# SyncE's queue in written order from the third pass on, and down's first load of h at the first product of the pass's last pair

## The chip, the cores and the metric

The kernel runs on one core of a Trainium2 chip. The metric is the device time of one execution in microseconds (us): 2458.67 us, median of three runs (2456.48 to 2459.65). Five engines work from their own queues: TensorE (PE; its weight loads are PEld), VectorE (DVE), ScalarE (ACT), GpSimd (POOL) and SyncE (SP). SP issues every DMA of this kernel.

## The reference, cut to what matters

```
S, D, H, Dh, F = 2048, 1024, 32, 32, 3584
xn = layernorm(x)
q, k, v = split(xn @ wqkv)                       # per head
phi(u) = concat(softmax(u @ w_phi), softmax(-(u @ w_phi)))
kv, z = phi(k)^T v, sum of phi(k) over s
o = (phi(q) kv) / (phi(q) z + 1e-6);  s = o @ wo
h = silu(xn @ w1) * (xn @ w3);        g = silu(h @ w2)
out = x + s * g
```

## The kernel before, in words

All large products are in float32 kept as two parts (a rounded high part and the rest, made by `split`, ACT for the high part and then DVE for the rest), and take three matmuls each (`PASSES`). Every 2 x 2 block product is done with seven block products, A11, A12, S2, S1, S3, S4 and A22, whose left operands are blocks of one matrix and sums of them, and whose right operands are called B11, B21, T2, T1, T3, B22 and T4.

The stages are, in order of time:

- up (to about 1175 us): h for all tokens, written to `h_d`.
- Three passes (c = 0, 1, 2; up to about 1683 us) over eight pairs of token tiles: keys and values for c = 0 and 1, queries for c = 2. A pair is seven products of 12 matmuls. `reload` brings the next pair's seven operands (tiles `xo`, L522). In the third pass `spikes` takes maxima, differences and an exponential of each result and stores it to `e_d` (L696, or L723 for two tiles, pairs 3 and 5, that are also scaled here with the tile `ee`).
- down (about 1673 to 2219 us): g = silu(h @ w2), loop `for r, new in enumerate(steps)`. Its contraction is cut in seven parts (kb = 0 to 6), and each part runs over the eight pairs (i = 0 to 7). Step r is 8 kb + i, 56 of them. `load_b(kb, n)` brings the nth right operand in two halves (tiles `bo` and `late`, L803, 512 KB each, in a ring of 24). `a_first(kb, i)` loads that step's h (tile `hr`, L810, 512 KB) and makes the high and low parts `af` (for A11 and A12) and `as2` (for S2); `a_second` makes those for S1, S3, S4 and A22 (`as`) from the same `hr`.
- In turn r of that loop PE does S1 of step r-1, A11 of r, S3 of r-1, A12 of r, S4 of r-1, S2 of r and A22 of r-1, 6 matmuls each. DVE adds each result to the accumulators `acc` (L987); A11 goes through ACT and POOL instead (L984, L985).
- In the last part (kb = 6, steps 48 to 55) `gate` applies Silu to each finished pair's two tiles on ACT (L918) and stores them (`g_d`, L919). The same turns load the weights and tiles of the last stage (`wos` L913, `zb` L731, `e` L931).
- The last stage (to 2454 us) puts s together and writes out.

What sets the order: within `in_order(...)` the named engines get their instructions as the code writes them. Outside it a scheduler places them, engine by engine, by its own costs. Up runs in order. Passes and down run scheduled on all engines until `new is None` (after step 55), from where SP, ACT, DVE and POOL are in order again, and in the last stage PE too. Whatever made the order, each engine's queue then runs strictly in it: an instruction that waits holds those behind it.

Of the kernel before, what the change touches and what calls it, by code (L numbers as in the profile page):

```python
# [28 lines left out]
def tile_kernel(ctx: ExitStack, tc: tile.TileContext, x, wkT, wqT, wv, wphi, wo, w1, w3, w2, out):  # L29
# [3 lines left out]
    def pool(name, bufs, **kw):  # L33

        open_pools[name] = tc.tile_pool(name=name, bufs=bufs, reuse_waits="tile", **kw)
        return open_pools[name].__enter__()

    def close(*names):
        for name in names:
            open_pools.pop(name).__exit__(None, None, None)  # L40

    ENG = mybir.EngineType
# [3 lines left out]
    def in_order(*engines):  # L46

        if ordered:
            ordered.pop().__exit__(None, None, None)
        if engines:  # L50
            ordered.append(tc.manual_schedule(engines=set(engines)))
            ordered[0].__enter__()
# [36 lines left out]
    def split(hi, lo, src, by=None):  # L89

        nc.scalar.copy(hi, src)  # L91
        (by or nc.vector).tensor_sub(lo, src, hi.bitcast(F))  # L92
# [66 lines left out]
    def fetch(m, j):  # L159
        t = slot(m, j)  # L160
        if m < 2:
            n = ANAMES[j]
            for q in range(4):
                nc.sync.dma_start(t[:, :, :, q * P:(q + 1) * P].bitcast(F), xo_d[m][n][:, q])
        else:
            n = BNAMES[j]
            nc.sync.dma_start(t.bitcast(F), wkv_d[m - 2][n])
        return {n: t}

    def quad(name, dt=R):  # L170
        return qp.tile([P, 2, 4, P], dt, name=name, tag="q")
# [345 lines left out]
    def reload(i, names=ANAMES):  # L517

        xo = {}
        for n in names:  # L520
            xo[n] = quad(f"xo{n}")
            nc.sync.dma_start(xo[n].bitcast(F), xo_d[i // 4][n][:, i % 4])  # L522
        return xo
# [107 lines left out]
    def seven(xo, wb):  # L631

        bank = {}
        for b, an, bn in ORDER:
# [8 lines left out]
            yield an, bank[b]  # L643

    def heads(i, xo, wb, steps, pend):

        nonlocal pkv
        first, last = i == 0, i + 1 == len(pairs)
        for an, pb in seven(xo, wb):
# [23 lines left out]
            else:  # L673
# [4 lines left out]
                kv(pkv, first, False, e0, v0)  # L678
                keys(pb, e1)
            next(steps)  # L680
        return pkv, False, last, e1, v1

# [46 lines left out]
    def load_z(two):  # L729
        for c in range(2):  # L730
            nc.sync.dma_start(two[c], z_d[:, c].rearrange("o g j s f -> o (g j s f)").to_broadcast([P, D]))  # L731

    def queries(i, xo, wb, steps, pend):

        t0, t1 = pairs[i]
# [51 lines left out]
    def ring(name):  # L787
        nonlocal ring_at
        k = ring_at % 24
        ring_at += 1  # L790
        if k < 8:
            return bpa.tile([P, 2, 512], R, name=name, tag=f"ra{k}")
        if k < 20:
            return bpb.tile([P, 2, 512], R, name=name, tag=f"rb{k}")
        return late_rw[(k - 20) // 2][:, k % 2]
# [3 lines left out]
    def load_b(kb, n):  # L799
        n = BNAMES[n]  # L800
        for kk in range(2):
            t = ring("bo")
            nc.sync.dma_start(t.bitcast(F), w2_d[kb][n][:, kk])  # L803
            bos[kb, n, kk] = t

    def a_first(kb, i):


        hq = quad("hr", F)
        nc.sync.dma_start(hq.rearrange("p b k t -> p (b k t)"),  # L810
                          h_d[i // 4][kb][i % 4].rearrange("p b h k t -> p (b h k t)"))
        hr = hq.rearrange("p b (h k) t -> p b h k t", h=2)
        sm = work.tile([P, 2, P], F, name="sm", tag="w")
        f1, f2 = quad("af"), work.tile([P, 2, 2, P], R, name="as2", tag="w")
        nc.vector.tensor_sub(sm, hr[:, 1, 0], hr[:, 0, 0])
        split(f1[:, 0], f1[:, 1], hq[:, 0])
        split(f2[:, 0], f2[:, 1], sm)
        return hq, sm, {"A11": (f1, 0), "A12": (f1, 2), "S2": (f2, 0)}

    def a_second(hq, sm, _):  # L820
        hr = hq.rearrange("p b (h k) t -> p b h k t", h=2)
        s34 = work.tile([P, 4, P], F, name="s34", tag="w")
        nc.vector.tensor_sub(s34[:, 0:2], hr[:, 1, 1], sm)
        nc.vector.tensor_sub(s34[:, 2:4], hr[:, 0, 1], sm)
        t1, t2 = quad("as"), quad("as")
        split(t1[:, 0], t1[:, 1], hq[:, 1])
        split(t2[:, 0], t2[:, 1], s34)
        return {"S1": (t1, 0), "A22": (t1, 2), "S3": (t2, 0), "S4": (t2, 2)}
# [3 lines left out]
    def split_wo(step):  # L832

        if step == 0:
            wso["room"] = [big.tile([P, 8, 512], F, name="room", tag=f"big{j}") for j in range(2)]
        for m in range(16):
            room, at_ = wso["room"][m % 4 // 2], 3 * (m % 2)
            raw_w, two = room[:, at_], room[:, at_ + 1:at_ + 3].bitcast(R)
            c, k = m // 8, m % 8
            if step == 2 * m:  # L840
                nc.sync.dma_start(raw_w, wo[k * P:(k + 1) * P, c * 512:(c + 1) * 512])
            elif step == 2 * m + 3:
                split(two[:, 0], two[:, 1], raw_w)
            elif step == 2 * m + 5:
                nc.sync.dma_start(wo_d[c][k], two.bitcast(F))
# [7 lines left out]
    ready = []  # L853
    for c in range(3):
        wbn = {}
        if c == 2:
            close("spare")
            bpa = pool("ra", 1, side="right")
        for i in range(len(pairs)):
            nxt, end = {}, i + 1 == len(pairs)  # L860

            def steps():
                for j in range(7):
                    if c == 0 and 4 <= 7 * i + j < 40:
                        split_wo(7 * i + j - 4)
                    if j == 0:
                        if i + 2 == len(pairs) and c < 2:
                            for m in range(2):
                                wbn.update(fetch(c + 3, m))
                        if not (end and c == 2):  # L870
                            nxt.update(reload((i + 1) % len(pairs)))
                        if c == 2 and i in (1, 2):
                            load_b(0, i - 1)
                        if c == 2 and end:
                            load_b(0, 2)
                            load_b(0, 3)
                    if later:
                        later.pop(0)()

                    if end and c < 2:  # L880
                        if j < 4 or (j == 4 and c == 0):
                            wbn.update(fetch(c + 3, j + 2))
                        if j == 6 and c == 1:
                            wbn.update(fetch(c + 3, 6))
                    if end and c == 2 and j in (1, 4):
                        ready.append(a_first(0, 0) if j == 1 else a_second(*ready[0]))
                    yield

            pend = (queries if c == 2 else heads)(i, xo, wb, steps(), pend)
            assert not (end and later)  # L890
            xo = nxt
        wb = wbn
# [101 lines left out]
    for r, new in enumerate(steps):  # L994
        kb, i = new or (NKB, 0)
        end = kb == NKB - 1
# [19 lines left out]
        if 8 <= r < 24:  # L1016
            c, j, s = (r - 8) // 8, (r - 8) // 2 % 4, r % 2
# [173 lines left out]
```

## Time and profile before

| | us |
|---|---|
| median of three runs | 2458.67 (2456.48 to 2459.65) |
| the profiled execution, its own time | 2455.73 |
| its span, first to last instruction | 2453.9 |
| mean granted TensorE clock | 0.995 |
| PE busy | 2380.6 (97%) |
| DVE busy | 1684.7 (69%) |
| ACT busy | 902.5 (37%) |

Idle time of PE is what is to be looked at first, since PE is busy for 97% of the span. In a timeline row the bracket tells how long the engine sat idle before it and what ended that; `x12` counts the merged instructions. A row of SP (SPq) is a DMA's issue, not its transfer.

### The profile page before, as it was taken

Reading aid. Unit: us, or ns where it says so; the run is one execution under the profiler, and the core shown is the slowest. Engines: PE = TensorE matmul, PEld = TensorE weight load, DVE = VectorE, ACT = ScalarE, POOL = GpSimd, SP = SyncE. Lnnn points to the kernel's source line nnn. Section 1 sums busy time; section 2 is a strip of 40 time slices with the busy share of each in tenths; the row PEclk is TensorE's granted clock in tenths of the full one; section 3 lists DMA queues with packets and bytes.
Section 4 is the critical chain, followed back from the end, with each engine's and each line's share of the span. In section 5 each row is a group of like instructions: output and inputs, shape, how many; then the busy total and the mean of one; then the engine's idle time right before and its main releaser. Section 6 shows DMA issues by size and latency. Waiting matters only on the chain.

```text
span 2453.9 us, 35828 instructions
## 1 busy us (share of the span) xinstructions
PE 2380.6 (97%) x13554; PEld 1951.1 (80%) x13554; DVE 1684.7 (69%) x2493; ACT 902.5 (37%) x1566; POOL 716.9 (29%) x511
## 2 busy tenths in 40 slices
PE   6999999999999999999999999998999999999999
PEld 5888877788777888878788788886888888887887
DVE  8556777775467777774476565695688787876764
ACT  6444544443344555443121111333422222243221
POOL 1233454543345565542000000010011111124653
PEclk9999999999999999999999999999999999999999
DMA  7566688966886777765998867978433444366553
GB/s 262 174 222 224 222 269 294 299 228 207 264 275 240 264 272 262 253 244 180 386 333 329 338 217 298 374 282 300 175 123 109 173 179 172 140 244 243 189 186 112
DMA packets 289548, 586.30 MB, mean 239 GB/s; under 512 B 23648, under 2 KB 138592, under 8 KB 286688
## 3 DMA queue, kind: packets, MB, share of 16 engines
q1 hardware_dynamic: 289376, 584.02, 68.2%
q8 instruction: 107, 1.75, 0.3%
q14 instruction: 65, 0.53, 0.1%
HBM read 379.19 MB, written 205.00 MB: 238 GB/s over the span
## 4 chain that ended last, share of the span: by engine, by line
PE 74%; DMA 9%; DVE 6%; issue 5%; POOL 3%; SPq 2%; ACT 1%; DVEq 0%; ACTq 0%; POOLq 0%
PE bankb L557 18%; PE bankb L975 12%; PE bankb L640 10%; PE bankc L557 8%; PE bankc L975 6%; PE banka L557 5%; PE bankc L640 5%; PE banka L975 3%; PE banka L640 2%; PE pm L1095 2%; DVE bo L92 1%; POOL ez L936 1%; POOL e L962 1%; DMA wkv_d0T<-wkvo 1%; PE pkv L626 1%
## 5 line engine op out<-in xcount | busy, mean ns | idle before, releaser
L92 DVE TENSOR_TENSOR bo<-rw,bo 128x512 fp32r<-128x512 f32 x336 | 292.6, 872 | 145.0 <-ACT bo L91 144.4
L91 ACT CAST bo<-rw 128x512 fp32r<-128x512 f32 x336 | 205.8, 621 | 49.8 <-DMA wkv_d0T<-wkvo 5.7
L985 POOL TENSOR_TENSOR acc<-acc,u 128x512 f32<-128x512 f32 x48 | 62.6, 1304 | 491.4 <-ACT u L984 491.4
L975 PE MATMUL bankb<-bo,as 128*128 128x512 f32 x816 | 200.9, 389 | 0.0
L269 POOL TENSOR_TENSOR rw<-rw,t 128x512 f32<-128x512 f32 x56 | 79.2, 1413 | 382.0 <-DVE bo L92 382.0
L1095 PE MATMUL pm<-wos,oT 128*128 128x512 f32 x768 | 183.0, 394 | 0.0
L975 PEld LDWEIGHTS bankb<-bo,as 128*128 128x128 f32 x816 | 153.2, 188 | 31.8
L557 PE MATMUL bankb<-op1A,bo 128*128 128x512 f32 x672 | 161.2, 396 | 11.5 <-DVE u L585 7.9
L557 PE MATMUL bankb<-op0A,bo 128*128 128x512 f32 x672 | 160.1, 392 | 8.6 <-DVE u L585 8.3
L1095 PEld LDWEIGHTS pm<-wos,oT 128*128 128x128 f32 x768 | 141.9, 188 | 31.7 <-issue 2.8
L557 PE MATMUL bankc<-op0S,bo 128*128 128x512 f32 x672 | 163.4, 391 | 2.0 <-ACT u L583 1.5
L557 PE MATMUL bankb<-op0S,bo 128*128 128x512 f32 x672 | 163.4, 392 | 1.8 <-ACT u L576 1.6
L557 PE MATMUL bankc<-op1S,bo 128*128 128x512 f32 x672 | 161.8, 390 | 1.6 <-ACT u L583 1.6
L557 PE MATMUL bankb<-op1S,bo 128*128 128x512 f32 x672 | 161.5, 389 | 0.0
L557 PEld LDWEIGHTS bankb<-op1A,bo 128*128 128x128 f32 x672 | 127.2, 191 | 42.4 <-DVE u L585 11.8
L557 PEld LDWEIGHTS bankb<-op0A,bo 128*128 128x128 f32 x672 | 125.1, 188 | 37.5 <-DVE u L585 11.4
L557 PEld LDWEIGHTS bankc<-op1S,bo 128*128 128x128 f32 x672 | 125.9, 188 | 28.8 <-ACT u L583 2.4
L557 PEld LDWEIGHTS bankc<-op0S,bo 128*128 128x128 f32 x672 | 125.2, 188 | 29.1 <-ACT u L583 2.4
L975 PE MATMUL bankc<-bo,as 128*128 128x512 f32 x576 | 146.6, 389 | 1.8 <-DMA bo<-w_d0B 1.8
L557 PEld LDWEIGHTS bankb<-op0S,bo 128*128 128x128 f32 x672 | 125.0, 188 | 29.0 <-ACT u L576 3.3
L557 PEld LDWEIGHTS bankb<-op1S,bo 128*128 128x128 f32 x672 | 126.0, 188 | 26.6 <-ACT u L576 0.4
L975 PEld LDWEIGHTS bankc<-bo,as 128*128 128x128 f32 x576 | 108.0, 188 | 24.9 <-DMA bo<-w_d0B 2.2
(241 smaller groups left out, 4683.4 us busy)
## 6 DMA issues: line engine op xcount, KB each, us to landing
rw<-in_w SPq DMA_DIRECT2D x112, 512.0 KB, 4.7
h_d<-h SPq DMA_DIRECT2D x112, 256.0 KB, 7.2
hr<-h_d SPq DMA_DIRECT2D x56, 512.0 KB, 3.6
xoS<-xo_d0S SPq DMA_DIRECT2D x48, 512.0 KB, 8.7
xoS<-xo_d1S SPq DMA_DIRECT2D x48, 512.0 KB, 7.7
xoA<-xo_d0A SPq DMA_DIRECT2D x36, 512.0 KB, 7.3
xoA<-xo_d1A SPq DMA_DIRECT2D x36, 512.0 KB, 5.8
e<-e_d SPq DMA_DIRECT2D x32, 512.0 KB, 4.3
```

What stands on the lines that cost most here:

```text
L91: nc.scalar.copy(hi, src)
L92: (by or nc.vector).tensor_sub(lo, src, hi.bitcast(F))
L269: nc.gpsimd.tensor_sub(b11, b22, t2)
L557: nc.tensor.matmul(bank[b], bo[bn][:, w, k], ao[an][:, u, k], start=first and n == 0, stop=LAST[b] == an and n == 11, skip_group_check=True)
L626: nc.tensor.matmul(pkv[sl, m], e[:, m // 4, (m % 4) * P + 32 * h:(m % 4) * P + 32 * h + 32], v[:, 4 * (m % 4) + h], start=first and m == 0 ...
L640: nc.tensor.matmul(bank[b], xo[an][:, u, k], wb[bn][:, w, k], start=an in ("A11", "A12", "S1") and n == 0, stop=LAST[b] == an and n == 11, ...
L936: nc.gpsimd.tensor_mul(t, es[i][c], zb[c])
L962: eng.tensor_mul(e3, e3, f.rearrange("p h s -> p (h s)").unsqueeze(2).to_broadcast([P, H, DH]))
L975: nc.tensor.matmul(bank[b], t[:, u, pos + k], bos[kb, bn, k][:, w], start=first and n == 0, stop=LAST[b] == an and n == 5, skip_group_chec ...
L985: nc.gpsimd.tensor_add(c, c, u)
L1095: nc.tensor.matmul(p, oT[k // 4][:, a, k % 4], wos[c, k][:, b], start=n == 0, stop=n == 23)
```

## The change

It puts SP, and SP alone, in written order from the start of the third pass. Since nothing ends that before `new is None`, it holds for all of down too. In the last pair of the third pass it writes step 0's load of h behind the first product instead of the second, and the loads of B right operands 2 and 3 (T2 and T1) behind the third and fourth instead of the first. The loads of operands 4 to 6 (T3, B22, T4) stay where they were written: behind the pass.

```
     for c in range(3):
         if c == 2:
+            in_order(ENG.SP)
             close("spare")
...
-                        if c == 2 and end:
-                            load_b(0, 2)
-                            load_b(0, 3)
+                    if c == 2 and end and j in (2, 3):
+                        load_b(0, j)
...
-                    if end and c == 2 and j in (1, 4):
-                        ready.append(a_first(0, 0) if j == 1 else a_second(*ready[0]))
+                    if end and c == 2 and j in (0, 4):
+                        ready.append(a_first(0, 0) if j == 0 else a_second(*ready[0]))
```

The scheduler, seeing another queue on SP, also orders ACT, DVE and PE anew. Three places matter.

SP around the end of the third pass, before. `e_d` are stores of the pass, of which `e_d_0_182` is the sixth pair's last and `e_d_0_176`, `1_185`, `1_177` and `0_184` are the last pair's four. `w_d0T_204`, `0T_205`, `0T_206`, `0B_207`, `0T_208` are T2, T1, T3, B22 and T4 of kb = 0.

```order
L696 DMA e_d_0_182<-eq 128x1024
L803 DMA bo<-w_d0T_204 128x1024 x2
L803 DMA bo<-w_d0T_205 128x1024 x2
L696 DMA e_d_0_176<-eq 128x1024
L810 DMA hr<-h_d_0_57 128x1024
L1019 DMA kvu_d<-kv_d_252 32x4x32 x8
L810 DMA hr<-h_d_0_57 128x1024 x2
L696 DMA e_d_1_185<-eq 128x1024
L803 DMA bo<-w_d0T_206 128x1024 x2
L696 DMA e_d_1_177<-eq 128x1024
L696 DMA e_d_0_184<-eq 128x1024
L803 DMA bo<-w_d0B_207 128x1024 x2
```

The first `hr` is step 0's, the next two are those of steps 1 and 2. And now:

```order
L696 DMA e_d_0_182<-eq 128x1024
L810 DMA hr<-h_d_0_57 128x1024
L696 DMA e_d_0_176<-eq 128x1024
L803 DMA bo<-w_d0T_204 128x1024 x2
L803 DMA bo<-w_d0T_205 128x1024 x2
L696 DMA e_d_1_185<-eq 128x1024
L696 DMA e_d_1_177<-eq 128x1024
L696 DMA e_d_0_184<-eq 128x1024
L803 DMA bo<-w_d0T_206 128x1024 x2
L803 DMA bo<-w_d0B_207 128x1024 x2
L803 DMA bo<-w_d0T_208 128x1024 x2
L810 DMA hr<-h_d_0_57 128x1024 x2
```

Step 0's `hr` moved up past four right-operand loads and a store. Those of steps 1 and 2 moved down, behind the pass's last store and six right-operand loads. The small `kvu_d` copies went further down, one to each turn.

SP in the turns of kb = 6, now. The first `hr<-h_d_6_63 x2` are the loads for steps 49 and 50, and the single one behind them that for step 51; `g_d_71` and `75` are the two tiles of the pair of step 48, `g_d_72` and `76` those of step 49.

```order
L810 DMA hr<-h_d_6_63 128x1024 x2
L919 DMA g_d_71<-acc_14244 128x1024
L919 DMA g_d_75<-acc_14245 128x1024
L913 DMA wos<-wo_d_0_186 128x1024
L913 DMA wos<-wo_d_1_187 128x1024
L913 DMA wos<-wo_d_2_188 128x1024
L913 DMA wos<-wo_d_3_189 128x1024
L731 DMA zb<-z_d 128x1024 x2
L810 DMA hr<-h_d_6_63 128x1024
L919 DMA g_d_72<-acc_14287 128x1024
L919 DMA g_d_76<-acc_14288 128x1024
L913 DMA wos<-wo_d_4_190 128x1024
```

Before, all three loads (steps 50, 51 and 52) stood ahead of `g_d_71`, mixed with the `wos`. Now the `hr` of step 51 stands behind the stores of step 48's pair, four `wos` and two `zb`, and in the same way that of step 52 behind the stores of step 49's pair and that of step 53 behind step 50's.

ACT in the same turns, before. `af` with its number is the high part for one step's A11: 18033 is step 51, 18122 step 52. `acc0` and `acc4` are the pair of step 48, `acc1` and `acc5` that of step 49.

```order
L91 CAST af_18033<-hr_18030 128x512
L91 CAST as2_18034<-sm_18032 128x256
L91 CAST as_18097<-hr_17941 128x512
L918 ACTIVATE acc0_14242<-acc0_14242 128x1024
L91 CAST as_18098<-s34_18094 128x512
L918 ACTIVATE acc4_14243<-acc4_14243 128x1024
L984 COPY u_18055<-bankb_18048 128x512
L91 CAST af_18122<-hr_18119 128x512
L91 CAST as2_18123<-sm_18121 128x256
L91 CAST as_18186<-hr_18030 128x512
L918 ACTIVATE acc1_14285<-acc1_14285 128x1024
L91 CAST as_18187<-s34_18183 128x512
```

And now, where `af_18035` is step 51's and `af_18124` step 52's, and `acc2` and `acc6` are the pair of step 50:

```order
L918 ACTIVATE acc4_14245<-acc4_14245 128x1024
L984 COPY u_18057<-bankb_18050 128x512
L918 ACTIVATE acc1_14287<-acc1_14287 128x1024
L918 ACTIVATE acc5_14288<-acc5_14288 128x1024
L91 CAST af_18035<-hr_18032 128x512
L91 CAST as2_18036<-sm_18034 128x256
L91 CAST as_18099<-hr_17943 128x512
L91 CAST as_18100<-s34_18096 128x512
L984 COPY u_18146<-bankb_18139 128x512
L918 ACTIVATE acc2_14366<-acc2_14366 128x1024
L918 ACTIVATE acc6_14367<-acc6_14367 128x1024
L91 CAST af_18124<-hr_18121 128x512
```

Step 51's cast stood ahead of the Silu of step 48's pair and now stands behind that of step 49's, whose second tile is complete only with A22 of step 49, the last product of turn 50. In the same way step 52's stands behind step 50's pair, and step 54's behind step 52's; steps 53 and 55 are not so placed. DVE's parts of these steps moved with them: they stand behind the adds of that same A22.

## The prediction

> **What bounds the kernel now.** I read the page's head first, then PE's waits from the third pass to the end of down, then the timelines of PE, SP, ACT and DVE round those waits, and the turns of kb = 6.
>
> ```profile
> span 2453.9 us, 35828 instructions
> PE 2380.6 (97%) x13554; PEld 1951.1 (80%) x13554; DVE 1684.7 (69%) x2493; ACT 902.5 (37%) x1566; POOL 716.9 (29%) x511
> ...
> PE bankb L975 <- ACT af L91: 9.1, 1, 9.1
> ...
> PE bankc L975 <- DMA bo<-w_d0B: 1.8, 1, 1.8
> ```
>
> PE is the bound, and down's products (L975) wait twice (us in total, times, longest): 9.1 us for the first `af`, 1.8 us for a right operand. Down has no third wait, so what the change can win there is small, and any new wait adds to the end.
>
> ```profile
> 1661.10 2.88 PE L640 MATMUL bankc<-op4T,xoS 128*128 128x512 f32 x12
> 1673.04 0.79 PE L975 MATMUL bankb<-bo,af 128*128 128x512 f32 x1 [9.07 <-ACT af L91]
> 1673.83 4.32 PE L640 MATMUL bankb<-op4T,xoS 128*128 128x512 f32 x12
> 1677.99 2.91 PE L640 MATMUL bankc<-op4B,xoS 128*128 128x512 f32 x12
> 1680.73 2.88 PE L640 MATMUL bankb<-op4T,xoA 128*128 128x512 f32 x12
> 1683.45 1.30 PE L975 MATMUL bankb<-bo,af 128*128 128x512 f32 x5
> ...
> 1696.50 2.57 PE L975 MATMUL bankc<-bo,as 128*128 128x512 f32 x10 [1.77 <-DMA bo<-w_d0B]
> 1698.90 1.07 PE L975 MATMUL bankb<-bo,af 128*128 128x512 f32 x4
> ...
> 646.88 8.40 PE L557 MATMUL bankb<-op1A,bo 128*128 128x512 f32 x24 [3.64 <-DMA op1A<-xo_d1A]
> 655.12 2.88 PE L557 MATMUL banka<-op1A,bo 128*128 128x512 f32 x12
> ```
>
> Columns are start, length, engine, line. From 1680.73 to 1683.45, 12 matmuls take 2.72 us: 0.227 each, 1.36 for six, 9.52 for a turn of seven sixes. After the 9.07 us gap the first product took 0.79 instead of 0.23 and the next twelve 4.16 (1673.83 to 1677.99) instead of 2.72: 2.0 us of low clock on top. The 3.64 us gap shows the same: 24 matmuls took 8.24 us (646.88 to 655.12) instead of 5.44, so 2.8 more. Behind the 1.77 us gap ten took 2.4 (1696.50 to 1698.90), so nothing was lost there.
>
> **1. The first load of h.**
>
> ```profile
> 1641.34 0.39 SPq L522 DMA_DIRECT2D xoA<-xo_d1A  x1
> 1643.96 0.32 SPq L723 DMA_DIRECT2D e_d<-ee  x1
> ...
> 1657.97 4.25 SPq L803 DMA_DIRECT2D bo<-w_d0T  x4
> 1664.49 0.32 SPq L696 DMA_DIRECT2D e_d<-eq  x1
> 1664.91 0.38 SPq L810 DMA_DIRECT2D hr<-h_d  x1
> ...
> 1672.99 1.42 SPq L810 DMA_DIRECT2D hr<-h_d  x2
> 1683.14 1.15 SPq L803 DMA_DIRECT2D bo<-w_d0T  x2
> 1686.36 3.04 SPq L696 DMA_DIRECT2D e_d<-eq  x2
> 1689.45 1.16 SPq L803 DMA_DIRECT2D bo<-w_d0B  x2
> ...
> DMA to landing us min/median/max: 7.4/7.4/7.4
> ...
> 2140.00:2144.00 4.00, 4.00 (x19) 3.32 (x18) 2.31 (x5) 2.14 (x4) 1.29 (x1) 1.00 1.02 418
> ```
>
> The landing line is that of step 0's `hr`: issued at 1664.91, in at 1672.3. It stood behind four `bo` loads issued from 1657.97. The window's last columns are granted clock, DMA share and GB/s: with the DMA engines full, 418 GB/s move, so 512 KB take 1.25 us. With the change `hr` goes where the first `bo` went, and four loads, 4 x 1.25 = 5.0 us, are no longer ahead of it: 1667.3. Against that, written order puts the last pair's two `xoA` loads (one is the 1641.34 row) behind the `ee` store of 1643.96, which brings 2 x 1.25 = 2.5 us of transfers later into the same queue: 1669.8 at worst. I take 1669.2, near the later end, since the queue is full there: 3.1 us gained. The bounds: issue at 1657.97 with the same 7.4 us gives 1665.4, a gain of 6.9, and then the gap left (2.2) is near the one of 1.77 that cost no clock, so 2.0 more, 8.9. The other end is 0. At 1669.2 the gap is still 6 us and the low clock stays. **-3.1 (-8.9 to 0).**
>
> What is late next: `hr` of step 0 is pulled forward, but everything that SP issued around it goes back.
>
> **2. Steps 0 and 1 behind the pass.** Before, the loads of `hr` for steps 1 and 2 went out at 1672.99, and T3 at 1683.14, ahead of the pass's last two stores (1686.36). Now T3, B22, T4 (six halves) and then `hr` of step 1 stand behind the last store, and a store waits for DVE and ACT:
>
> ```profile
> 1686.31 0.68 DVE L692 TENSOR_TENSOR eq<-bankb,mm 128x512 f32<-128x512 f32 x1
> 1686.90 0.68 DVE L693 TENSOR_TENSOR eq<-mm,bankb 128x512 f32<-128x512 f32 x1
> ...
> 1687.99 1.07 ACT L694 ACTIVATE eq<-eq 128x1024 f32<-128x1024 f32 x1
> ...
> hr<-h_d SPq DMA_DIRECT2D x56, 512.0 KB, 3.6
> ...
> DMA to landing us min/median/max: 7.0/7.0/7.0
> ```
>
> Let P be the end of the pass's last product (1683.45 before). Behind it DVE has four instructions for the last tile, which the order puts straight behind an add and four others for the tile before, whose result is complete at P - 2.72. At 0.6 us from start to start these nine reach P + 2.9, the exponential (1.07) ends near P + 4.1, the store goes out at P + 4.25, T3's first half at P + 4.65 by SP's 0.4 per issue. It lands 5.0 later, my choice between 3.6 (the median of all `hr`, as the page lists it) and 7.0 (the landing line, that of `bo` at 1689.45): P + 9.65. Five more halves at 1.25: P + 15.9. `hr` of step 1: P + 17.15, its cast 0.65: P + 17.8. PE's order has step 0's 41 open matmuls ahead of step 1's A11. Before, 41 took 41 x 0.227 + 1.77 = 11.1 from P. So **+6.7**, PE standing at S3 from P + 5.2 for 4.4 us and then waiting for each half. The low clock that this gap may bring falls on matmuls that wait for a half anyway. Bounds: first landing 3.6, +5.4; 7.0, +8.8.
>
> **3. The turns of kb = 6.**
>
> ```profile
> 2155.42 3.02 SPq L919 DMA_DIRECT2D g_d<-acc  x2
> ...
> 2162.91 2.88 PE L975 MATMUL bankb<-bo,as 128*128 128x512 f32 x12
> 2165.63 1.52 PE L975 MATMUL bankc<-bo,as 128*128 128x512 f32 x6
> ...
> 2150.05 0.62 ACT L91 CAST af<-hr 128x512 fp32r<-128x512 f32 x1
> ...
> 2166.55 1.06 ACT L918 ACTIVATE acc<-acc 128x1024 f32<-128x1024 f32 x1
> ...
> 2165.83 0.69 DVE L987 TENSOR_TENSOR acc<-bankb,acc 128x512 f32<-128x512 f32 x1
> ...
> 2172.38 0.69 DVE L92 TENSOR_TENSOR as<-hr,as 128x512 fp32r<-128x512 f32 x1
> ```
>
> Turn 50 ends with A22 of step 49, whose six are the second half of the row at 2162.91, and turn 51 starts at 2165.63 with no gap. Before, `af` of step 51 was cast at 2150.05, 17 us ahead of its use. In the new order that cast stands on ACT behind the Silu of step 49's second tile. That tile is complete when DVE has added A22 (2165.83, 0.69), the Silu runs at 2166.55 for 1.06, then the cast, 0.62: 2168.2, and with it the halves for S1 of step 50, which the order puts behind it. PE can't start turn 51 at 2165.63: a wait of 2.6 us. DVE's parts of the set stand behind the same add, and neither engine can pass what waits.
>
> For step 51 the load is later still. Its `hr` stands behind both `g_d` (the second out at about 2158.1: the row's first at 2155.42, two in 3.02), four `wos` and two `zb`: seven transfers at 1.25 ahead of it, and 3.6 for itself, 2170.4; with the cast, 2171.0, a wait of 5.4 us, which is past 3.64 and halves the clock for 24 matmuls, 2.1 to 2.8 more; I take 2.1: +7.5. If those transfers run faster, the floor is 2.6. Step 52: the same chain without a late load, +2.6. Step 54: the same, plus one DVE instruction (0.69 less hand-off) that stands ahead of S1's low half: +3.2. Steps 53 and 55 have no such order, 0, covered by the two turns that their casts stand ahead. **Sum +13.3, at least 8.4.** Above: a low clock at 52 and 54, +5.6.
>
> The Trainium skill ("TensorE: Matmul & The Clock Gate", section "HAM oscillation — how this bites in real kernels") gives the rule that PE gaps over about 3.4 us bring the throttle back. Here 3.64 us did and 1.77 us didn't, which agrees; no row lies between. By that rule the gaps of 2.6 and 3.2 us stay at full clock and the sum is as I have it; if gaps of 2.6 are enough, it is the third rival.
>
> **4. Third pass.** The `xoA` loads of pairs 5 and 7 stand behind a scaled store. `xoA` lands in 5.8 us at the median, and pair 7's second, then issued near 1646, would be in at 1652, about when it is needed:
>
> ```profile
> 1652.93 2.88 PE L640 MATMUL bankb<-op4B,xoA 128*128 128x512 f32 x12
> xoA<-xo_d1A SPq DMA_DIRECT2D x36, 512.0 KB, 5.8
> ```
>
> +0.5 for both pairs together (0 to 1.7, as many as DVE's scaling comes late).
>
> Nothing else moves to the path: `kvu_d` is small and used in the last stage; the loads at the other kb boundaries come one turn later but PE has 9.5 us a turn and `hr` lands in 3.6; the last stage was in order before.
>
> **Sum.** -3.1 + 6.7 + 13.3 + 0.5 = +17.4 against the profiled execution's own 2455.73 (its span 2453.9 and 1.8 around it): 2473.1. The median of the runs is 2458.67, 2.9 above it, so **2476** against that. What a measurement can tell from no change here is about 0.2%, 4.9 us.
>
> **Rivals.**
>
> A, faster: the early `hr` is worth the whole of the entry, 9.07 + 2.0 = 11.1 us, and the new order costs only step 2's floor of 5.4, because the gate turns don't wait. 2458.67 - 5.7 = 2453.0. It decides where all new waits stay below 11.1 - 4.9 = 6.2. For it: the entry's gap is the largest in the second half, and DMA is the only thing ahead of `hr`. Against: 1657.97 + 7.4 leaves 2.2 of the gap, and ACT's and DVE's rows in the gate turns are in strict order. Chance 0.07.
>
> B, the same within 0.2%: the entry wins 8.9, step 2 costs 5.4, and of the gate turns only step 51 waits (7.5), since the other casts have slack that I can't see: +4.0, 2462.7. For it: `hr` is the only load that is shown late; against: A22 is the turn's last product, so a Silu of its tile can't be earlier. Chance 0.12.
>
> C, larger loss: each new gap also drops the clock, 2 x 2.8 at steps 52 and 54, and 2 in step 2 behind the first gap: 17.4 + 7.6 = 25.0, 2483.7. For it: the bound between 1.77 and 3.64 isn't known. Chance 0.17.
>
> The forecast with its own range (2467 to 2481) has 0.64. The range 2461 to 2486 takes in B, the forecast and C; what it leaves out is A and the outer ends of B and C, together about 0.18. Slower by over 0.2%: the forecast and C, 0.81; same 0.12; faster 0.07.
>
> **What would show it.** Right: the wait for the first `af` near 6 us instead of 9.07; PE waiting for `bo` (T3) behind the pass, then for `af` of step 1; waits for `af` or `as` at the start of the turns of steps 51, 52 and 54, the first the longest with `hr` as its releaser through ACT. Wrong: kb = 6 without a wait (step 3 falls, and with it the sign may turn), step 1's A11 within P + 12 (step 2 falls), or a first gap under 2.5 us.

## The result and the profile after

The changed kernel took 2490.34 us, median of four runs (2489.64 to 2492.04), against 2457.57 us (2455.08 to 2459.65) for four runs of the kernel before: ratio 1.0135, 95% interval 1.0117 to 1.0152. It is slower, as forecast, but by 32.8 us instead of 17.4, and outside the range.

The head of the page, and PE's waits from the third pass to the end of down (us in total, times, longest):

```profile
span 2490.3 us, 35806 instructions
...
PE bankb L975 <- ACT af L91: 20.6, 5, 7.8
PE bankb L975 <- DMA bo<-w_d0T: 6.1, 3, 5.2
PE bankc L975 <- DVE as L92: 3.9, 1, 3.9
```

Down had two waits and now has nine in these three groups; the largest is again the wait for `af`, now five times. Where they lie, in PE's timeline:

```profile
1671.91 0.80 PE L975 MATMUL bankb<-bo,af 128*128 128x512 f32 x1 [5.28 <-ACT af L91]
1672.69 5.18 PE L640 MATMUL bankb<-op4T,xoS 128*128 128x512 f32 x12
...
1683.17 1.29 PE L975 MATMUL bankb<-bo,af 128*128 128x512 f32 x5
...
1693.91 2.90 PE L975 MATMUL bankb<-bo,as 128*128 128x512 f32 x6 [5.22 <-DMA bo<-w_d0T]
...
1702.97 0.73 PE L975 MATMUL bankb<-bo,af 128*128 128x512 f32 x2 [1.38 <-ACT af L91]
...
2173.20 2.88 PE L975 MATMUL bankb<-bo,as 128*128 128x512 f32 x12
2183.92 1.22 PE L975 MATMUL bankb<-bo,af 128*128 128x512 f32 x2 [7.84 <-ACT af L91]
...
2193.42 2.88 PE L975 MATMUL bankb<-bo,as 128*128 128x512 f32 x12
2198.68 0.73 PE L975 MATMUL bankb<-bo,af 128*128 128x512 f32 x2 [2.38 <-ACT af L91]
...
2223.42 1.19 PE L975 MATMUL bankb<-bo,af 128*128 128x512 f32 x2 [3.71 <-ACT af L91]
...
2229.75 2.08 PE L975 MATMUL bankc<-bo,as 128*128 128x512 f32 x4 [3.85 <-DVE as L92]
```

The first wait fell from 9.07 to 5.28 us. Behind the pass PE stands at S3 (5.22) and at A11 of step 1 (1.38). In kb = 6 it stands at the start of the turns of steps 51, 52 and 54, and in the last of these twice.

The ledger below is worked out from the starts of matmuls in each trace: the third pass's first product, the pass's end, down's 144th matmul, its 2017th (the fifth product of the turn of step 48), its 2311th (the same place in the turn of step 55), the span's end. So each of the seven turns in the fourth column runs from the middle of one turn of kb = 6 to the middle of the next, and holds the start of the later one. It begins at the third pass because the same code ahead of it took 1517.4 to 1526.9 us in the twelve profiles, which is more than most of the effects. Each row is one execution; kernels with the same code in a column agree within 1.6 us there, so smaller differences say nothing.

| us | third pass | to the 144th | to the 2017th | to the 2311th: kb = 6 | rest | sum | against before |
|---|---|---|---|---|---|---|---|
| before | 166.04 | 34.51 | 424.55 | 66.64 | 244.77 | 936.50 | |
| after | 163.68 | 42.91 | 426.16 | 93.33 | 244.69 | 970.77 | +34.3 |
| SP in order in the pass only | 163.42 | 33.55 | 424.55 | 66.64 | 244.74 | 932.88 | -3.6 |
| moved loads only | 157.19 | 39.47 | 424.55 | 66.64 | 244.65 | 932.49 | -4.0 |
| order only | 171.05 | 42.10 | 426.08 | 91.13 | 244.68 | 975.03 | +38.5 |
| h two steps ahead | 163.75 | 41.98 | 424.85 | 76.41 | 244.76 | 951.75 | +15.3 |
| late e stores | 159.69 | 33.13 | 424.55 | 66.64 | 244.73 | 928.74 | -7.8 |
| g store a turn later | 164.65 | 41.87 | 424.75 | 69.45 | 244.89 | 945.61 | +9.1 |
| one e pair later | 164.03 | 42.05 | 424.57 | 82.83 | 244.75 | 958.24 | +21.7 |
| h before two more stores | 155.64 | 37.31 | 424.55 | 66.64 | 244.73 | 928.87 | -7.6 |
| h of two steps early | 155.62 | 34.45 | 424.55 | 66.64 | 244.79 | 926.04 | -10.5 |
| three stores late | 156.04 | 33.39 | 424.55 | 66.64 | 244.73 | 925.35 | -11.2 |

Of the 34.3 us, -2.4 are the third pass, +8.4 the steps behind it, +1.6 the boundaries between parts of down, and +26.7 the turns of kb = 6. Nothing is lost or gained behind that.

### The profile page after: what moved, and what is told of

It reads as the page before. It is cut to its first block, busy times and chain, and to the rows that moved or that the text cites. A ratio compares the mean times of both kernels' runs of the same rounds, so it can differ in the third digit from the quotient of the medians.

```text
span 2490.3 us, 35806 instructions
## 1 busy us (share of the span) xinstructions
PE 2393.1 (96%) x13554; PEld 1956.0 (79%) x13554; DVE 1691.6 (68%) x2493; ACT 901.9 (36%) x1566; POOL 724.3 (29%) x511
## 4 chain that ended last, share of the span: by engine, by line
PE 71%; DMA 11%; DVE 6%; issue 5%; POOL 4%; ACT 2%; SPq 1%; DVEq 0%; ACTq 0%; POOLq 0%
PE bankb L557 19%; PE bankb L975 11%; PE bankb L640 10%; PE bankc L557 8%; PE bankc L975 6%; PE banka L557 5%; PE bankc L640 4%; PE banka L975 3%; PE banka L640 2%; DMA hr<-h_d 2%; POOL ez L936 2%; PE pm L1095 2%; DVE bo L92 2%; POOL e L962 1%; PE pkv L626 1%
## 5 line engine op out<-in xcount | busy, mean ns | idle before, releaser
L985 POOL TENSOR_TENSOR acc<-acc,u 128x512 f32<-128x512 f32 x48 | 64.7, 1348 | 516.4 <-ACT u L984 479.3
L557 PE MATMUL bankb<-op1A,bo 128*128 128x512 f32 x672 | 160.3, 394 | 10.9 <-DVE u L585 7.9
L987 DVE TENSOR_TENSOR acc<-bankb,acc 128x512 f32<-128x512 f32 x152 | 104.5, 687 | 57.5 <-PE bankb L975 54.4
```

Of the source, the lines that this page charges most:

```text
L557: nc.tensor.matmul(bank[b], bo[bn][:, w, k], ao[an][:, u, k], start=first and n == 0, stop=LAST[b] == an and n == 11, skip_group_check=True)
L985: nc.gpsimd.tensor_add(c, c, u)
L987: nc.vector.tensor_add(c, pb, c)
```

## The experiments

The theory: nearly all of the loss is SP's written order inside down, where it puts loads behind stores that wait for ACT and DVE, and the scheduler, knowing that, puts ACT's and DVE's casts behind the Silu; the moved loads by themselves are a small gain. Rivals: the written order in the third pass costs by itself; the moved loads cost; in kb = 6 only the late load counts, or only the casts' place. Each ratio below is against runs of the kernel before that were made beside it.

**Written order in the third pass alone.** The order ends with the pass.

```
         wb = wbn
+    in_order()
     close("big")
```

> SP's written order ends with the third pass; down is scheduled again, the moved loads stay. Theory (the loss is SP's written order within down: 26.1 us in the turns of kb = 6, 1.9 at kb boundaries, most of 8.6 behind the pass, since the loads of h for steps 1 and 2 go ahead of the pass's last stores again): the gate turns run without a wait, 9.52 us each, the wait for the first af stays near 5.3 us, and the time is 2451 to 2458, at or under the kernel before. Rival (written order in the third pass costs by itself, through the xoA loads and the late e_d stores): the steps behind the pass still lose 5 us or more and the time is 2462 or more.

Measured: 2457.15 us against 2458.44, ratio 0.9992 (0.9982 to 1.0002), and from the third pass on 3.6 us shorter. PE's waits from the third pass to the end of down:

```profile
PE bankb L976 <- ACT af L91: 5.5, 1, 5.5
...
PE bankb L976 <- DMA bo<-w_d0T: 0.7, 1, 0.7
```

All turns of kb = 6 take 9.52 us again, and the steps behind the pass 33.55 (34.51 before). The first wait stays at 5.5. The rival falls for all that lies behind the pass; what the order costs within the pass, the next run shows.

**The moved loads alone.** No written order at all.

```
         if c == 2:
-            in_order(ENG.SP)
             close("spare")
```

> Only the moved loads; SP is scheduled everywhere. Theory: no wait in kb = 6, first load of h issued ahead of the four right-operand loads as in the changed kernel, first wait 4 to 7 us, time 2450 to 2459. Rival (the scheduler puts the loads back where it wants them, so the moves do nothing without the written order): first wait 9 us again and 2457 to 2459.

Measured: 2455.83 us against 2458.44, ratio 0.9987 (0.9977 to 0.9997).

```profile
1669.79 0.74 PE L974 MATMUL bankb<-bo,af 128*128 128x512 f32 x2 [1.38 <-ACT af L91]
...
1693.66 0.93 PE L974 MATMUL bankb<-bo,as 128*128 128x512 f32 x3 [1.45 <-DMA bo<-w_d0T]
...
1697.37 1.22 PE L974 MATMUL bankb<-bo,af 128*128 128x512 f32 x2 [1.19 <-ACT af L91]
```

The scheduler put the load ahead of the four `bo`, with the `xoA` loads left early, so the first wait is 1.38 us (4 to 7 expected) and brings no low clock: the third pass is 8.9 us shorter, my far bound for it, and 6.2 shorter than with the written order. 5.0 are given back behind the pass, in waits of 1.45 us and less and in a low clock that they brought together (0.50 from 1695.3 to 1702.1). So the moves don't need the written order, which costs a good part of their gain; that it does so through the `xoA` loads is read from SP's rows, not tried alone.

**The written order alone.** The loads of h, T2 and T1 go back to where they were written.

```
-                    if c == 2 and end and j in (2, 3):
-                        load_b(0, j)
+                        if c == 2 and end:
+                            load_b(0, 2)
+                            load_b(0, 3)
...
-                    if end and c == 2 and j in (0, 4):
+                    if end and c == 2 and j in (1, 4):
```

> Only SP's written order; the first load of h and the loads of T2 and T1 where they were. Theory: all the losses of the changed kernel (about 8.6 behind the pass, 26 in kb = 6) and none of its gain at the entry: first wait 9 to 12 us, time 2491 to 2498. Rival (the loss comes from the moved loads, which the order only carries through): 2470 or less.

Measured: 2495.77 us, ratio 1.0152 (1.0137 to 1.0167). First wait 12.38 us (9 to 12 expected), and 42.10 and 91.13 us in the ledger's second and fourth columns, as in the changed kernel (42.91, 93.33). So the moved loads add at most 3 us to the loss in these two columns; the order alone gives the rest.

**Loads of h two turns ahead in kb = 6.**

```
             first = a_first(*steps[r + 1])
+            if end and r + 2 < len(steps) - 1:
+                a_load(*steps[r + 2])
```

(`a_load` is the load out of `a_first`, which then takes the tile that was loaded.)

> The changed kernel with the loads of h for steps 50 to 55 written one turn earlier, so ahead of the stores of the pair two steps back. The order still has ACT's casts behind the Silu of the finished pair. Theory (two causes in kb = 6: the late load, about 5 us in turn 51 and 3 to 4 in turn 54 with the low clock that follows, and the casts' place behind the Silu): the waits for the load go, those of 2.4 to 3 us behind the Silu stay, kb = 6 loses 8 to 16 us instead of 26, time 2474 to 2484. Rival (it is the late load alone): kb = 6 loses under 3 us, time 2464 to 2468. Rival (the casts' place alone): the loss stays above 22 us, 2487 or more.

Measured: 2475.54 us, ratio 1.0071 (1.0054 to 1.0089). kb = 6 loses 9.8 us instead of 26.7, inside the forecast of two causes. But the waits aren't those that I named. Two of PE's, with what DVE did ahead of them:

```profile
2201.64 1.66 PE L981 MATMUL bankc<-late,as 128*128 128x512 f32 x6 [1.02 <-DVE acc L993]
...
2223.06 1.80 PE L981 MATMUL bankc<-late,as 128*128 128x512 f32 x6 [2.57 <-DVE acc L993]
...
2200.56 0.43 DVE L821 TENSOR_TENSOR sm<-hr 128x256 f32<-128x256 f32 x1 [2.00 <-DMA hr<-h_d]
...
2219.81 2.59 DVE L821 TENSOR_TENSOR sm<-hr 128x256 f32<-128x256 f32 x1
```

DVE stood on a later set's subtraction, in the first case because its h wasn't there, in the second because that instruction took 2.59 us instead of 0.4, beside a product on GpSimd that started at 2219.77; the add that frees PE's bank was behind it. So an engine in order that waits for a load holds up other work too. One turn's lead for the loads is worth 17 of the 26.7 us; the other 10 are not split further by this run.

**The stores of g a turn later.** `gate` only notes its tiles; the stores are written behind the next `a_first`.

```
             nc.scalar.activation(acc[t], acc[t], AF.Silu)
-            nc.sync.dma_start(g_d[t], ...)
+            stores.append(t)
...
             first = a_first(*steps[r + 1])
+        store_g()
```

> The changed kernel with the stores of g written one turn later, behind the next load of h; nothing else. Theory (in kb = 6 written order ties Silu, its store and the next load of h into one chain; the load is late because it stands behind a store that waits for A22, and the casts were placed behind the Silu because of that chain): with the store one turn later the casts go back ahead of the Silu, kb = 6 loses 0 to 5 us instead of 26.7, time 2463 to 2469. Rival (it is the number of transfers ahead of the load, four wos and two zb, not the store): turn 51 still waits 4 us or more, kb = 6 loses over 12 us, 2476 or more.

Measured: 2468.16 us against 2460.73, ratio 1.0033 (1.0019 to 1.0046); kb = 6 loses 2.8 us, and what is left is a wait of 2.31 in the turn of step 55. `wos` and `zb`, six of the eight transfers that stood ahead of step 51's load, still do, so their number is not the cause: it is the store that waits for Silu, which waits for A22. In the order, the cast for step 51 is back ahead of the Silu of step 49's pair. So the late load and the casts' place went together, and no run separates what each costs.

**One pair of e loads later.** So two transfers instead of four stand ahead of step 54's h, and GpSimd's products with that e run later.

```
             elif i == 4:
                 load_e(1)
-                load_e(2)
+            elif i == 6:
+                load_e(2)
```

> The changed kernel with one pair of e loads written behind the last load of h: two transfers fewer ahead of step 54's h (2.5 us), and GpSimd's two products with that e no longer beside DVE's set for step 54. Theory (turn 54's 11.1 us are 3.9 for h behind four e loads, 3.9 for DVE slowed while GpSimd works, and the low clock behind both): turn 54 loses 2.5 to 5 us, DVE's subtraction there takes 0.4 us again instead of 2.6, the other turns unchanged, time 2482 to 2486 if the last stage doesn't wait for the e, which may give back 1 to 4. Rival (GpSimd's work beside DVE costs nothing, the gap is the late h alone): DVE's wait of 3.9 us stays.

Measured: 2481.78 us against 2460.73, ratio 1.0088 (1.0074 to 1.0102). The seventh with the start of step 54's turn takes 11.14 us instead of 20.58, so it loses 1.6 where I expected 2.5 to 5; the others stay (51: 19.67, 52: 13.81), and the rest of the kernel does not give anything back. Its PE and DVE rows:

```profile
2219.64 0.74 PE L975 MATMUL bankb<-bo,af 128*128 128x512 f32 x2 [1.27 <-ACT af L91]
...
2220.62 0.42 DVE L824 TENSOR_TENSOR s<-hr,sm 128x256 f32<-128x256 f32 x1
2220.95 0.68 DVE L92 TENSOR_TENSOR as<-hr,as 128x512 fp32r<-128x512 f32 x1
```

L824 takes 0.42 us again (2.58 in the changed kernel, rows below) and PE doesn't wait a second time. The two transfers and GpSimd's work were moved at once, and the scheduler put step 54's cast ahead of the pair's second Silu, so how much each is worth alone isn't separated, but the two rows show that the second wait went with GpSimd's work.

**A version that keeps the gain.** Four kernels without written order, with the moved loads. First, the last pair's last two stores of e are written behind step 1:

```
+        if hold:
+            held.append(lambda: nc.sync.dma_start(e_d[t][c], e))
+            return
...
         if r == 1:
+            while held:
+                held.pop(0)()
             late_rw += ...
```

> Only the moved loads, SP scheduled (as the run of the moves alone), and the pass's last two stores of e written behind step 1, so that T3, B22, T4 and the load of h for step 2 don't stand behind them. In the run of the moves alone the entry gained 8.9 us and the steps behind the pass lost 5.0 of it. Theory (those 5.0 come from the loads' place behind stores that wait for DVE and ACT, at P + 4): the waits behind the pass go to under 1.5 us, third pass to end 7.5 to 10 us shorter than before, time 2447 to 2452. Rival (the DMA engines are full there, so the loads land as late wherever they stand): no change against the moves alone, 2453 to 2457.

Measured: 2451.35 us against 2460.73, ratio 0.9966 (0.9953 to 0.9979). The steps behind the pass take 33.13 us instead of 39.47, so they had waited in the main for the stores' turn in the queue: the two stores' own transfers, at 1.25 us each, could account for 2.5 of the 6.3 us at most. The third pass came out at 159.69 instead of 157.19, with a first wait of 2.23 and a low clock behind it.

Then the last two stores of the pair before (i = 6) too, released behind step 0's load of h:

```
-   hold = i + 1 == len(pairs)
+   hold = i + 2 >= len(pairs)
...
+                    if end and c == 2 and j == 0:
+                        while held:
+                            held.pop(0)()
```

> As the run with the late stores, and the sixth pair's last two stores of e written behind step 0's load of h, two transfers (2.5 us) fewer ahead of it. Theory: the first wait goes from 1.4 us to 0 and the entry is 10 to 11 us shorter than before, but the load of h for step 1 now stands behind T4 in the order, which costs 2 to 4 us behind the pass: 2447 to 2453. Rival (the first wait is not the load's any more): no change against the run with the late stores.

Measured: 2452.40 us, ratio 0.9970 (0.9958 to 0.9981). No first wait, third pass 155.64 (10.4 shorter than before), and 37.31 behind it, with this last wait:

```profile
1690.51 0.73 PE L980 MATMUL bankb<-bo,af 128*128 128x512 f32 x2 [1.39 <-ACT af L91]
```

Then step 1's load of h written in the last pair, and beside it the same kernel with one store more of that pair, the third, held back:

```
+                    if end and c == 2 and j == 3:
+                        a_load(0, 1)
```

> The run before with the sixth pair's last two stores behind step 0's load of h, and step 1's load of h written in the pass's last pair, ahead of T3 (there it stood behind T4 and was the last wait, 1.4 us, behind the pass). Theory: entry as there, 155.6 us from the third pass's first product to the pass's end, and 33.5 to 36 us for the next 143 products instead of 37.3, so third pass to end 925 to 927.5 us against 936.5 before; time 2447 to 2451. Rival (the DMA engines are full, moving a load up moves T3 to T4 down by the same): 928 to 929 again, 2451 to 2453.

```
-                spikes(t1, 1, d1, e01[:, 1])
+                spikes(t1, 1, d1, e01[:, 1], hold=i + 1 == len(pairs))
```

> As the run beside it, and one more of the last pair's stores of e behind step 1, so that T3's loads wait for no store. Theory: T3 lands 1 to 3 us earlier and what is left of the waits behind the pass goes: next 143 products 32.6 to 34.5 us, third pass to end 924 to 926.5 us, time 2446 to 2450. Rival (T3's loads wait for room that the pass's products free at its end, not for the store): as the run beside it.

Measured on one chip: 2449.73 and 2450.08 us against 2459.51, ratios 0.9965 (0.9951 to 0.9978) and 0.9962 (0.9949 to 0.9974). The two can't be told apart by time, so the rival for the third store (no difference) stands; in the ledger they are 10.5 and 11.2 us shorter than before. Of the last one, PE's waits from the third pass to the end of down are, for down:

```profile
PE bankb L988 <- ACT af L91: 1.6, 2, 1.2
```

The 9.07, its low clock and the 1.77 us of the kernel before are gone but for 1.6.

## Why the prediction was right in sign and wrong in size

**Step 1, the first load of h (-3.1), and step 4 (+0.5): right.** Together -2.6 forecast, -2.4 measured. The queue of loads was as full as I took it to be:

```profile
1648.28 0.32 SPq L723 DMA_DIRECT2D e_d<-ee  x1
1648.69 0.38 SPq L696 DMA_DIRECT2D e_d<-eq  x1
1649.17 1.85 SPq L522 DMA_DIRECT2D xoA<-xo_d1A  x2
...
1661.44 0.32 SPq L810 DMA_DIRECT2D hr<-h_d  x1
...
1671.23 0.62 ACT L91 CAST af<-hr 128x512 fp32r<-128x512 f32 x1 [1.14 <-DMA hr<-h_d]
```

Both `xoA` loads stand behind the scaled store, and `hr`, issued at 1661.44, is cast at 1671.23, nearly 10 us later; I had 1669.2 for its landing, and this execution came to the third pass 2.1 us later. The low clock stayed, and cost 0.9 more than before (twelve matmuls took 5.02 us, 1672.69 to 1677.71, instead of 4.16). So the sum's agreement is in part luck: the wait fell by 3.8 and not 3.1, and the dearer low clock took most of that back. Step 4's 0.5 is there, in small waits for the late `xoA` at 1617.20 and 1655.49.

**Step 2, behind the pass (+6.7): mechanism right, 1.7 short, inside its bounds (5.4 to 8.8).** With P = 1683.17:

```profile
1682.23 5.83 SPq L696 DMA_DIRECT2D e_d<-eq  x3
1688.16 1.15 SPq L803 DMA_DIRECT2D bo<-w_d0T  x2
...
1691.80 1.19 SPq L810 DMA_DIRECT2D hr<-h_d  x2
```

T3's first half goes out at P + 5.0 (4.65 forecast) and PE starts S3 at 1693.91, P + 10.7 (9.65). A11 of step 1 starts at P + 19.8 (17.8). From its issue to PE's start T3's first half took 5.75 us where I had chosen 5.0, and step 1's h, behind the other five halves, another 1 us more than I had.

**Step 3, the turns of kb = 6 (+13.3): the places right, the sum half of what it was, 26.7.** This is the step that failed, and it failed in three terms. By turns: 10.7 at that of step 51, 4.3 at 52, 11.1 at 54, and 0.6 at the end of that of 48.

The load of step 51 came later than seven transfers and 3.6 us (from the second store of g to its landing 14.8 us, where I had 12.3):

```profile
2166.25 2.47 SPq L919 DMA_DIRECT2D g_d<-acc  x2
2168.82 2.17 SPq L913 DMA_DIRECT2D wos<-wo_d  x4
2171.09 1.20 SPq L731 DMA_DIRECT2D zb<-z_d  x2
2172.34 0.64 SPq L810 DMA_DIRECT2D hr<-h_d  x1
...
DMA to landing us min/median/max: 10.9/10.9/10.9
...
2183.25 0.62 ACT L91 CAST af<-hr 128x512 fp32r<-128x512 f32 x1 [5.36 <-DMA hr<-h_d]
```

The landing line is that of the `hr` issued at 2172.34: in at 2183.2, 7.3 us after PE could have started (2175.92, twelve matmuls behind 2173.20), where I had 4.8. So wait and low clock were 8.0 and 2.7 instead of 5.4 and 2.1.

The turn of step 52 waited as forecast (2.38 by the profile's row, 2.6 forecast), but the clock dropped, and the turn cost 1.8 us on top. The number after POOL's count is the granted clock:

```profile
2196.19:2199.60 3.41, 1.03 (x5) 0.76 (x5) 2.30 (x5) 2.40 (x4) 0.00 (x0) 1.00 0.56 232
2199.60:2203.01 3.41, 3.41 (x10) 2.68 (x9) 1.72 (x4) 0.97 (x2) 0.00 (x0) 0.50 0.70 229
```

That is my third rival's cause, which had 0.17, at one of its places; the turn of step 54 had a low clock too, but behind a gap of 3.71, longer than the rival's, and the one in step 2 fell, as I had said, on products that would have waited for a half. The Trainium skill ("TensorE: Matmul & The Clock Gate", section "HAM oscillation — how this bites in real kernels") puts the limit at gaps over about 3.4 us; here the measurement decides against it: 2.38 was enough. The last section shows what decided it. I had also written that no row lies between 1.77 and 3.64 us, which is wrong: the profile of before has a gap of 2.93 us near its start, with half the clock behind it, and would have pointed to the rival.

```profile
48.24 1.84 PE L246 MATMUL pw<-bd,wr 128*128 128x128 f32 x8 [2.93 <-DMA wr<-in_wkT]
...
48.47:51.88 3.41, 3.41 (x18) 3.41 (x18) 3.41 (x6) 3.09 (x7) 0.00 (x0) 0.50 0.96 273
```

The turn of step 54 I had at 2.6 + 0.6. Two things were missing. Its `hr` stands behind four loads of e, which the order showed and I did not count; and GpSimd's products slow DVE's part of the set:

```profile
2212.40 2.15 SPq L931 DMA_DIRECT2D e<-e_d  x4
2214.59 0.55 SPq L810 DMA_DIRECT2D hr<-h_d  x1
...
2222.75 0.42 DVE L815 TENSOR_TENSOR sm<-hr 128x256 f32<-128x256 f32 x1 [2.31 <-DMA hr<-h_d]
...
2224.36 2.58 DVE L824 TENSOR_TENSOR s<-hr,sm 128x256 f32<-128x256 f32 x1
2226.87 2.82 DVE L92 TENSOR_TENSOR as<-hr,as 128x512 fp32r<-128x512 f32 x1
...
2224.11 5.04 POOL L936 TENSOR_TENSOR ez<-e,zb 128x1024 f32<-128x1024 f32 x2 [9.15 <-DMA g_d<-acc]
```

A subtraction of the same shape (L823) takes 0.42 us at 2223.09, this one 2.58 beside GpSimd. The profile of before had the price already, off the path, so I could have found it:

```profile
2196.60 2.60 POOL L936 TENSOR_TENSOR ez<-e,zb 128x1024 f32<-128x1024 f32 x1 [7.00 <-ACT acc L918]
...
2196.86 2.90 DVE L92 TENSOR_TENSOR as<-hr,as 128x512 fp32r<-128x512 f32 x1
```

The Trainium skill ("SBUF — State Buffer", section "Who interferes with whom") says that a DVE instruction with two SBUF inputs contends with a GpSimd instruction that reads SBUF. The trace agrees: these have two SBUF inputs, while DVE's adds with a PSUM bank as one input kept 0.7 us (0.68 at 2201.37 in the profile of before, beside the product that GpSimd started at 2200.86).

**"Nothing else moves to the path": not quite.** The other boundaries of down cost 1.6 us, in waits of 0.36 and 0.67 (at 1847.86 and 1850.19 in PE's timeline) and what follows them. At the second of these, and in the 0.6 us of the turn of step 48, DVE's subtraction L824 took 1.52 us instead of 0.42 (at 1848.01 and 2153.20) beside GpSimd's add L985, and the add that frees PE's bank stood behind it; that this is the cause is read from the rows, not tried. Three runs with the same code in these parts lose there 0.0 to 0.3 (424.57 to 424.85 in the ledger), so it doesn't come with the order each time.

**The rivals.** A and B needed the turns of steps 52 and 54 to run without a wait, and A that of step 51 too; all three waited. C had the right sign and one of its causes, with too small a price, since the late loads and GpSimd were not in it.

## What to carry to other kernels

A queue that is put in written order ties each load to every store written ahead of it, and each store to the engine that makes its data: before doing that, walk through every load in the region, not only the one that is to move, and count all that stands ahead of it. A scheduler that knows the order will also move casts behind the work that feeds those stores, so the loss shows up on engines that were not touched. Here the gain lay in the moved load and in holding back four or five stores, without any written order.

## What was not expected of the hardware

- The length of a gap doesn't decide whether the clock drops behind it. 2.38 us in the changed kernel and 2.23 in the run with the late stores dropped it, 2.31 in the run with the g store a turn later didn't:

```profile
2221.04 1.20 PE L982 MATMUL bankc<-bo,as 128*128 128x512 f32 x4 [2.31 <-DVE as L92]
...
2216.79:2220.20 3.41, 1.94 (x9) 1.28 (x7) 3.41 (x6) 1.06 (x1) 0.84 (x1) 1.00 0.00 0
2220.20:2223.62 3.42, 2.58 (x11) 2.16 (x12) 3.33 (x6) 2.35 (x4) 1.00 (x1) 1.00 0.41 168
```

  The traces' clock records show what goes with a drop. In each of the twelve traces the granted clock changes only at instants that lie whole multiples of 3.413 us apart (146 changes, each within 0.001 us of that grid), and what it does at such an instant follows PE's busy time in the 3.413 us before it. Of 8476 such windows at full clock (from 24 us on, with PE's busy time as the profile has it), all 72 in which PE was busy for under 46% were followed by half the clock, none of the 8388 with 50% or more, and 1 of the 16 between. The clock came back behind the first window with over 81% (61 of 61; none of the 31 with less). The gap of 2.38 lies whole in one window (busy 1.03 of 3.41 us, rows further up); that of 2.31 lies across an edge, at 2220.20, and leaves both windows over half busy (1.94 and 2.58). So in the run of the moved loads a gap of 1.55 us at 1203.25, with short waits ahead of it, dropped the clock (busy 1.26 of 3.41), while 1.78 at 1199.80 in the kernel before didn't. All this is counted in the traces; no run was made to shift a gap against the edges.
- The price follows from it: half of the time in which PE works at the low clock. In the turn of step 51 that was from 2183.92 to the edge at 2189.36, 5.4 us, and half of it is the 2.7 measured; in that of step 52 one window of 3.41, and 1.7 of the 1.8.
- A load of 512 KB took 10.9 us from issue to landing with the queue full, three times the 3.6 us that the page lists as the median: in a full stretch the median of all loads is no estimate.
